# Fewer weight decodes in the retention stage, and w_in splits two chunks ahead

## The chip, the cores and the metric

The kernel runs on one core of one Trainium2 chip. The metric is device time in microseconds (us), the median of several executions. "The span" is the time from the first to the last instruction in a profiled execution.

## What is computed

Three layers, one after the other, on a batch of 4 sequences of 576 tokens (2304 tokens, 512 features):

```python
# retention: 8 heads of 64, gamma[h] = 1 - 2 ** (-5 - h)
scores = (q @ k.T) / 8                       # per batch and head
x = (scores * where(t >= s, gamma ** (t - s), 0)) @ v
x = x.transpose(0, 2, 1, 3).reshape(2304, 512)
# first feed-forward layer, w_in 512 x 2048, w_out 2048 x 512
x = relu(x @ w_in) ** 2 @ w_out
# second feed-forward layer
h = x @ w_in2
out = (h * clip(h + 3, 0, 6) / 6) @ w_out2   # output float32
```

q, k and v arrive as 32-bit floats, the four weight matrices as 64-bit floats, which the chip's engines don't compute with.

## The kernel before

**Decodes.** A weight matrix is cut into 16 chunks of 128 hidden columns. What the kernel calls a half is one chunk of one matrix, 512 KB of 64-bit words. `load_w` (L116) loads a half into a staging buffer: the first four halves have buffers of their own (t3 to t6), all later ones share three. `decode` (L132) makes 32-bit floats of it in three parts that the caller runs when it likes. The first part is two ScalarE conversions (L148, L149) and two VectorE operations (L150, L153); the second (L159) and third (L165) are VectorE's. Its two work buffers, a and r, are double. Decoded w_in chunks stay in w0 to w7, two chunks each; decoded w_out chunks go to a pool, wd.

**Splits.** Every matrix product on 32-bit floats is made of three fast ones: `split_to` (L169) writes a rounded high part (ScalarE) and the rest, the low part (VectorE or GpSimd), and TensorE runs high x high, high x low and low x high. `split_x` does that for the activations, `split_in` for a w_in chunk (into one of two buffers, q0 and q1), `split_out` for a w_out chunk.

**Retention.** 20 tiles of up to 128 tokens; the batches go in two pairs, so the tiles of index 0 to 9 are those of batches 0 and 1, and the last two of each pair have only 64 tokens. Per tile TensorE makes scores (aps, L212), an addition to the running state (sps, L233), and one tile later the values (vps, L252 and L259); VectorE masks the scores (ret, L219), adds the state (L241) and scales the result into xall (L264); GpSimd scales the tile's values (kvt, L196) and the state (L242). Five tiles' buffers are there, so the load of a tile is issued when the values of the tile five before it are done. All loads are issued by SP in the order of the program. Between the tiles, AHEAD = 8 halves of w_in are decoded: the first part in every second tile from index 2 on, the rest in the tile after it. The tile at index 11, 13, 15 and 17 also splits a quarter of the first x.

**First feed-forward layer.** 64 units: four groups of tokens (`FIRST`: 768, 512, 512, 512), 16 chunks in each. Unit i runs h = x @ w_in of its chunk (`emit_h`, 24 matmuls in the first group, 12 in the others), then g = relu(h)^2 with its split (`emit_g`), and the product with w_out of the chunk two before it (`y_steps`, LAG = 2). In the first group each unit also decodes one half of w_out and, in some units, one of w_in. The program's order on each engine is written out by hand: in a unit the decode's first part stands ahead of emit_g, the second inside it, the third behind. The loads' order is a list, `coming`; each finished decode issues the next load. In the first group h of a unit uses PSUM banks 6 and 7, which the unit before it also used, so its matmuls wait until ScalarE's ReLU (L349) has read them. Later units decode the second layer's weights (`ready_steps`) and store split weights to DRAM; the second layer (L533) follows.

## Time and profile before

| | us |
|---|---|
| median of 3 runs | 869.36 (865.73 to 869.61) |
| the profiled execution: device time | 866.37 |
| its span | 864.6 |
| TensorE busy in the span | 846.1 |
| VectorE busy | 546.3 |
| ScalarE busy | 446.8 |
| GpSimd busy | 160.2 |

The profile records one execution. PE is TensorE's matmuls, PEld its weight loads, DVE is VectorE, ACT ScalarE, POOL GpSimd, SP the queue that issues most DMAs. L12 is line 12 of the kernel. "out<-in" are the program's names of what an instruction writes and reads, "x16" the number of merged instructions. The bracket at the end of a line of the timeline is the idle time of the engine before it and what ended it. A wait for several things is put down to the one that came last. A line of the busy table has the stretch, its length, the busy time (with instructions) of PE, PEld, DVE, ACT and POOL, TensorE's granted clock as a share of full speed, the DMA engines' busy share and what they moved in GB/s. A line of the groups has busy time and mean ns of one after the first bar, idle time before them and what ended it after the second.

### The profile page before, as it was taken

How to read it: one execution, taken by the hardware profiler on the slowest of the kernel's cores; microseconds unless marked ns; L12 is line 12 of the kernel's file. 1: busy time of each engine (PE TensorE's matmuls, PEld its weight loads, DVE VectorE, ACT ScalarE, POOL GpSimd, SP SyncE). 2: the span in 40 equal slices, each digit the busy share in tenths (PEclk: the TensorE clock that was granted, in tenths of full speed). 3: DMA queues.
4: the chain of work that ended last, by engine and by line, in shares of the span. 5: the costliest groups of instructions: out<-in, count | busy, mean ns of one | idle time of the engine just before them, and what ended most of it. 6: DMA issues, size and time to landing. Idle time of an engine off the chain costs nothing.

```text
span 864.6 us, 13261 instructions
## 1 busy us (share of the span) xinstructions
PE 846.1 (98%) x4970; PEld 734.7 (85%) x4970; DVE 546.3 (63%) x888; ACT 446.8 (52%) x814; POOL 160.2 (19%) x137
## 2 busy tenths in 40 slices
PE   8987999999999999999999999999999999999998
PEld 6876788888888888888888889889989889889897
DVE  4998877765477877787675645456554455643533
ACT  1130877676576777777765533335433345433332
POOL 3444433433033313432240000000000000000000
PEclk9999999999999999999999999999999999999999
DMA  9993454545487688778768545545476453674431
GB/s 362 346 360 95 133 192 141 190 134 185 134 293 269 232 281 291 267 263 302 259 209 316 183 159 196 196 146 194 164 287 207 159 204 125 246 268 168 173 120 73
DMA packets 70576, 184.18 MB, mean 213 GB/s; under 512 B 10224, under 2 KB 26608, under 8 KB 70512
## 3 DMA queue, kind: packets, MB, share of 16 engines
q1 hardware_dynamic: 69936, 182.21, 59.9%
q10 hardware_dynamic: 576, 1.12, 0.3%
q8 instruction: 39, 0.64, 0.3%
q14 instruction: 25, 0.20, 0.1%
HBM read 147.14 MB, written 36.18 MB: 212 GB/s over the span
## 4 chain that ended last, share of the span: by engine, by line
PE 90%; DMA 4%; DVE 4%; ACT 1%; issue 1%; POOL 0%; SPq 0%; DVEq 0%; ACTq 0%; POOLq 0%
PE yps L513 23%; PE hps L329 22%; PE hps L547 20%; PE yps L372 20%; PE ytail L372 3%; DMA kvt<-in_kv_dram 2%; DVE ret L219 1%; DMA stage<-in_w_out_dram 1%; PE vps L252 1%; DVE xring L171 1%; DVE xall L264 1%; DMA cst<-in_consts_dram 1%; PE vps L259 0%; DVE a L159 0%; DVE w L165 0%
## 5 line engine op out<-in xcount | busy, mean ns | idle before, releaser
L513 PE MATMUL yps<-wo,g 128*128 128x512 f32 x864 | 226.2, 394 | 0.0
L372 PE MATMUL yps<-g,wo 128*128 128x512 f32 x768 | 194.2, 391 | 0.0
L513 PEld LDWEIGHTS yps<-wo,g 128*128 128x128 f32 x864 | 159.6, 188 | 23.6 <-DVE g L562 0.3
L372 PEld LDWEIGHTS yps<-g,wo 128*128 128x128 f32 x768 | 140.0, 188 | 24.9
L329 PE MATMUL hps<-xring,win 128*128 128x512 f32 (+1 forms) x720 | 153.7, 362 | 2.1 <-ACT r L349 2.1
L329 PEld LDWEIGHTS hps<-xring,win 128*128 128x128 f32 x720 | 123.2, 189 | 23.5 <-ACT r L349 2.3
L547 PE MATMUL hps<-xlast,win 128*128 128x384 f32 x576 | 116.1, 336 | 0.0
L547 PEld LDWEIGHTS hps<-xlast,win 128*128 128x128 f32 x576 | 103.2, 188 | 8.8
L171 DVE TENSOR_TENSOR g<-r,g 128x512 fp32r<-128x512 f32 x64 | 46.9, 733 | 82.6 <-ACT g L170 82.1
L566 DVE TENSOR_TENSOR u<-hps,u 128x384 f32<-128x384 f32 x48 | 26.8, 558 | 107.3 <-PE hps L547 107.3
L349 ACT ACTIVATE r<-hps 128x512 f32<-128x512 f32 x80 | 44.1, 552 | 95.5 <-PE hps L329 95.5
L547 PE MATMUL hps<-xop,win 128*128 128x384 f32 x432 | 87.2, 336 | 0.0
L547 PEld LDWEIGHTS hps<-xop,win 128*128 128x128 f32 x432 | 77.5, 188 | 6.6
L560 ACT ACTIVATE g<-c 128x384 fp32r<-128x384 f32 x72 | 37.8, 525 | 84.3 <-DVE c L559 84.3
L148 ACT ACTIVATE a<-stage 128x512 f32<-128x512 f32 x64 | 42.0, 656 | 45.7 <-DVE w L165 31.4
L558 ACT ACTIVATE v<-c,three 128x384 f32<-128x384 f32 x72 | 44.4, 617 | 32.6 <-DVE c L566 31.4
L329 PE MATMUL hps<-xown,win 128*128 128x512 f32 x240 | 59.8, 390 | 0.7 <-ACT xall L381 0.7
L150 DVE TENSOR_SCALAR a<-a 128x512 f32<-128x512 f32 x64 | 47.3, 739 | 10.3 <-ACT a L148 10.3
L329 PEld LDWEIGHTS hps<-xown,win 128*128 128x128 f32 x240 | 44.8, 188 | 10.1 <-ACT xall L381 0.9
L585 ACT ACTIVATE c<-hps 128x384 f32<-128x384 f32 x24 | 11.8, 492 | 76.4 <-PE hps L547 76.4
L170 ACT ACTIVATE win<-w 128x512 fp32r<-128x512 f32 x64 | 39.6, 619 | 21.4 <-PE vps L259 21.4
L559 DVE SCALAR_TENSOR_TENSOR c<-v,c 128x384 f32<-128x384 f32 x72 | 40.0, 555 | 13.7 <-ACT v L558 13.7
(75 smaller groups left out, 1042.8 us busy)
## 6 DMA issues: line engine op xcount, KB each, us to landing
wo<-kept SPq DMA_DIRECT2D x96, 512.0 KB, 5.1
win<-kept SPq DMA_DIRECT2D x72, 512.0 KB, 3.6
kept<-ready SPq DMA_DIRECT2D x40, 512.0 KB, 3.8
stage<-in_w_in_dram SPq DMA_DIRECT2D x32, 512.0 KB, 4.4
stage<-in_w_out_dram SPq DMA_DIRECT2D x32, 512.0 KB, 4.2
qkt<-in_qk_dram SPq DMA_DIRECT2D x16, 512.0 KB, 7.2
kvt<-in_kv_dram SPq DMA_DIRECT2D x16, 512.0 KB, 7.7
kept<-wo SPq DMA_DIRECT2D x16, 512.0 KB, 5.8
```

What stands on the lines that cost most here:

```text
L148: nc.scalar.activation(out=a, in_=high.bitcast(F32), func=ACTF.Abs)
L150: nc.vector.tensor_scalar(out=a, in0=a, scalar1=LEAST, scalar2=MOST, op0=ALU.max, op1=ALU.min)
L170: nc.scalar.activation(out=hi, in_=src, func=ACTF.Copy)
L171: lo_engine.tensor_tensor(out=lo, in0=src, in1=hi.bitcast(F32), op=ALU.subtract)
L329: nc.tensor.matmul(out=h, lhsT=w[:, wp, kk * 128:kk * 128 + 128], rhs=xs[pos, kk][xp][:, o:o + n], start=m == 0, stop=m == 3 * KD - 1,)
L349: nc.scalar.activation(out=r, in_=hs[k], func=ACTF.Relu)
L372: nc.tensor.matmul(out=p, lhsT=w[:, wp, m * 128:m * 128 + 128], rhs=g[pos, c][k][:, gpart, :size], start=c == 0 and e == 0 and not (k and ...
L513: nc.tensor.matmul(out=p, lhsT=gt[m // 3][:, gpart, m % 3 * 128:][:, :128], rhs=w[:, wp], start=first and e == 0, stop=last and e == 2,)
L547: nc.tensor.matmul(out=to, lhsT=wl[k][:, half, wp, o], rhs=x[:, xp, f], start=first and m == 0, stop=last and m == 5, skip_group_check=True,)
L558: nc.scalar.activation(out=v, in_=c, func=ACTF.Relu, bias=three)
L559: nc.vector.scalar_tensor_tensor(out=c, in0=v, scalar=6.0, in1=c, op0=ALU.min, op1=ALU.mult)
L560: nc.scalar.activation(out=hi, in_=c, func=ACTF.Copy)
```

## The change

- Five w_in halves are decoded in the retention tiles in place of eight: first parts at the tiles of index 4, 6, 8, 10 and 12. The other eleven follow in the units of the first group, at unit (c - 5) * 6 // 5 for chunk c.
- A decode has four parts: what was the first is now ScalarE's conversions alone, and VectorE's two operations on them are a part named clamp. In the retention tiles first and clamp run together as before. In the units, the first part is issued at the end of a unit and the rest in the next unit: w_out's at its start, that of w_in with clamp ahead of emit_g and the other two parts behind it.
- In emit_g, VectorE's low parts come after all of ScalarE's operations.
- w_in is split two units ahead in place of one: chunks 0 and 1 in the tiles of index 14 and 16, the others behind emit_g.
- Split of the second group's x comes behind emit_g in the last three units of the first group.
- The running states move from q0 to w3.
- Loads: the first five tiles are issued without halves between them, and a half follows each tile load in the tiles of index 1 to 7 (before: three halves among the first five tiles, one in each of the tiles of index 0 to 3).
- WARM, the number of matmuls on zeros at the start, goes from 26 to 18.

```diff
--- before.py
+++ after.py
@@ -33,9 +33,9 @@
 MOST = float(np.array(0x47EFFFFF, np.uint32).view(np.float32))
 LAG = 2
 
-AHEAD = 8
-
-WARM = 26
+AHEAD = 5
+
+WARM = 18
 
 READY = list(range(17, 59))
 
@@ -147,6 +147,8 @@
         def first():
             nc.scalar.activation(out=a, in_=high.bitcast(F32), func=ACTF.Abs)
             nc.scalar.activation(out=r, in_=low.bitcast(U32), func=ACTF.Copy, scale=2.0 ** -29)
+
+        def clamp():
             nc.vector.tensor_scalar(
                 out=a, in0=a, scalar1=LEAST, scalar2=MOST, op0=ALU.max, op1=ALU.min
             )
@@ -164,7 +166,7 @@
         def third():
             nc.vector.tensor_tensor(out=f.bitcast(I32), in0=a.bitcast(I32), in1=r, op=ALU.add)
 
-        return [first, second, third]
+        return [first, clamp, second, third]
 
     def split_to(hi, lo, src, lo_engine):
         nc.scalar.activation(out=hi, in_=src, func=ACTF.Copy)
@@ -173,7 +175,7 @@
 
     tiles = [(b, i, min(C, S - C * i)) for pair in range(0, B, 2) for i in range(NTB) for b in (pair, pair + 1)]
     data, rets = {}, {}
-    every = place("q0", [128, 2, 2, HP, D], F32, "state")
+    every = place("w3", [128, 2, 2, HP, D], F32, "state")
     states = [[every[:, k, j] for j in range(2)] for k in range(2)]
 
     def load_tile(ti):
@@ -336,8 +338,8 @@
 
     g, gtail = {}, []
 
-    def emit_g(pos, c, hs, between):
-        g[pos, c] = []
+    def emit_g(pos, c, hs):
+        g[pos, c], lows_g = [], []
         for k, (o, n) in enumerate(parts(pos)):
             r = cp.tile([128, 512], F32, tag="c", name="r")[:, :n]
             if k == 0:
@@ -348,11 +350,11 @@
                 gt = gtail[0][:, c % 3]
             nc.scalar.activation(out=r, in_=hs[k], func=ACTF.Relu)
             nc.scalar.activation(out=r, in_=r, func=ACTF.Square)
-            if k == 0:
-                for f in between:
-                    f()
-            split_to(gt[:, 0, :n], gt[:, 1, :n], r, nc.vector)
+            nc.scalar.activation(out=gt[:, 0, :n], in_=r, func=ACTF.Copy)
+            lows_g.append((gt[:, 1, :n], r, gt[:, 0, :n]))
             g[pos, c].append(gt)
+        for lo, src, hi in lows_g:
+            nc.vector.tensor_tensor(out=lo, in0=src, in1=hi.bitcast(F32), op=ALU.subtract)
 
     yb = {}
 
@@ -613,7 +615,7 @@
 
     halves = [(-1, 0, c, 0) for c in range(AHEAD)]
     halves += [(c, 0, c, 1) for c in range(NCH)]
-    halves += [((c - AHEAD) * 7 // 4, 0, c, 0) for c in range(AHEAD, NCH)]
+    halves += [((c - AHEAD) * 6 // 5, 0, c, 0) for c in range(AHEAD, NCH)]
     halves.sort(key=lambda x: x[0])
     coming = halves + [
         (0, 1, 2 * p + e, w) for p in range(NPAIR) for e, w in ((0, 0), (1, 0), (0, 1), (1, 1))
@@ -634,8 +636,6 @@
         load = lambda: load_w(*coming.pop(0)[1:])
         for ti in range(1, len(TOKENS)):
             load_tile(ti)
-            if ti > 1:
-                load()
 
         warm = bank(0, [128, 256], "warm")
         for _ in range(WARM):
@@ -656,10 +656,11 @@
                 scale_values(ti + 2)
             if ti:
                 values(ti - 1)
-            if ti < 4:
+            if 1 <= ti <= 7:
                 load()
-            if ti >= 2 and ti % 2 == 0 and halves[0][0] < 0:
+            if ti >= 4 and ti % 2 == 0 and halves[0][0] < 0:
                 decoding = decode(*halves.pop(0)[1:])
+                decoding.pop(0)()
                 decoding.pop(0)()
             elif decoding:
                 for f in decoding:
@@ -668,8 +669,8 @@
                 next_load()
             if ti in (11, 13, 15, 17):
                 split_x(0, (ti - 11) // 2)
-            if ti == len(tiles) - 2:
-                split_in(0, 0, nc.gpsimd)
+            if ti in (14, 16):
+                split_in(0, (ti - 14) // 2, nc.gpsimd)
         values(len(tiles) - 1)
         assert halves[0][0] >= 0 and len(xs) == KD and not decoding
         ring["from"] = 4
@@ -678,24 +679,35 @@
         ready = [f for p in range(NPAIR) for f in ready_steps(p)]
         pace, owed = sum(x[0] for x in ready) / len(READY), 0
         sums, highs, lows = operand_steps(0)
+        due = []
         for i, (pos, c) in enumerate(units):
-            dec = []
-            while halves and halves[0][0] <= i:
-                dec.append(decode(*halves.pop(0)[1:]))
             h = emit_h(pos, c)
-            if pos + 1 < len(FIRST) and c >= NCH - 3:
+            dec, due = due, []
+            for d in dec[:1]:
+                for f in d:
+                    f()
+                next_load()
+            for d in dec[1:]:
+                d.pop(0)()
+            if pos and pos + 1 < len(FIRST) and c >= NCH - 3:
                 for kk in ((0,), (1,), (2, 3))[c - NCH + 3]:
                     split_x(pos + 1, kk)
-            if i + 1 < len(units):
-                split_in(*units[i + 1], nc.gpsimd if pos == 0 else nc.vector)
+            emit_g(pos, c, h)
+            for d in dec[1:]:
+                for f in d:
+                    f()
+                next_load()
+            if pos == 0 and c >= NCH - 3:
+                for kk in ((0,), (1,), (2, 3))[c - NCH + 3]:
+                    split_x(pos + 1, kk)
+            if i + 2 < len(units):
+                split_in(*units[i + 2], nc.gpsimd if i + 2 < NCH else nc.vector)
             if 1 <= i <= NCH:
                 split_out(i - 1, nc.gpsimd)
-            for d in dec:
-                d[0]()
-            emit_g(pos, c, h, [d[1] for d in dec])
-            for d in dec:
-                d[2]()
-                next_load()
+            while halves and halves[0][0] <= i:
+                d = decode(*halves.pop(0)[1:])
+                d.pop(0)()
+                due.append(d)
             if i >= LAG:
                 for f in y_steps(*units[i - LAG]):
                     f()
```

## Rows read from the trace of the kernel before

**Rows 1.** The page, busy time and instructions of each engine, TensorE's line

```profile
PE 846.1 (98%) x4970; PEld 734.7 (85%) x4970; DVE 546.3 (63%) x888; ACT 446.8 (52%) x814; POOL 160.2 (19%) x137
```

**Rows 2.** Who waited for whom, TensorE: us in total, times, longest

```profile
PE sps L233 <- POOL kvt L196: 5.0, 6, 2.3
...
PE hps L329 <- ACT r L349: 2.1, 1, 2.1
```

**Rows 3.** Busy time by stretch, the last a chunk with two decodes

```profile
2.00:22.00 20.00, 17.14 (x219) 13.89 (x219) 8.74 (x17) 2.96 (x5) 7.34 (x9) 0.91 1.03 395
...
16.80:24.00 7.20, 6.10 (x94) 5.48 (x96) 2.61 (x6) 1.28 (x3) 3.23 (x4) 0.76 1.05 403
24.00:83.60 59.60, 51.39 (x895) 44.22 (x892) 57.64 (x92) 10.96 (x17) 28.55 (x28) 0.96 0.78 274
...
121.36:129.74 8.38, 8.38 (x51) 7.37 (x49) 6.80 (x10) 6.36 (x13) 2.87 (x3) 1.00 0.45 146
```

**Rows 4.** Timeline of TensorE: start us, us, then what

```profile
17.90 1.12 PE L233 MATMUL sps<-kvt 128*64 128x64 f32 x16 [2.30 <-POOL kvt L196]
...
62.07 1.16 PE L212 MATMUL aps<-qkt 64*128 64x128 f32 x16
63.16 0.69 PE L233 MATMUL sps<-kvt 128*64 128x64 f32 x16
63.68 1.04 PE L252 MATMUL vps<-ret,kvt 128*64 128x128 f32 x16
64.65 1.09 PE L259 MATMUL vps<-qkt,state 64*64 64x128 f32 x16
65.67 1.16 PE L212 MATMUL aps<-qkt 64*128 64x128 f32 x16
...
78.00 0.63 PE L212 MATMUL aps<-qkt 64*64 64x64 f32 x16
81.39 1.17 PE L252 MATMUL vps<-ret,kvt 64*64 64x64 f32 x15 [2.76 <-issue]
...
85.20 8.79 PE L329 MATMUL hps<-xring,win 128*128 128x512 f32 x48
```

**Rows 5.** Timeline of GpSimd, retention, fourth and eighth tile's values

```profile
16.80 1.04 POOL L196 TENSOR_TENSOR kvt<-kvt,cst 128x512 f32<-128x512 f32 x1 [3.66 <-DMA kvt<-in_kv_dram]
...
33.62 1.04 POOL L196 TENSOR_TENSOR kvt<-kvt,cst 128x512 f32<-128x512 f32 x1 [1.73 <-DMA kvt<-in_kv_dram]
```

**Rows 6.** Timeline of VectorE, retention, one decode and what follows

```profile
64.40 0.46 DVE L150 TENSOR_SCALAR a<-a 128x512 f32<-128x512 f32 x1
...
65.96 1.28 DVE L219 TENSOR_TENSOR ret<-aps,cst 128x512 f32<-128x512 f32 x2
...
68.08 0.72 DVE L159 SCALAR_TENSOR_TENSOR a<-stage,a 128x512 int32<-128x512 int32 x1
...
70.18 0.94 DVE L171 TENSOR_TENSOR xring<-xall,xring 128x768 fp32r<-128x768 f32 x1
```

**Rows 7.** Timeline of ScalarE in the first chunks, then TensorE's first y

```profile
88.42 0.60 ACT L349 ACTIVATE r<-hps 128x512 f32<-128x512 f32 x1 [0.18 <-PE hps L329]
...
91.47 0.62 ACT L170 ACTIVATE win<-w 128x512 fp32r<-128x512 f32 x1
...
93.19 0.66 ACT L148 ACTIVATE a<-stage 128x512 f32<-128x512 f32 x1
...
95.47 0.58 ACT L349 ACTIVATE r<-hps 128x512 f32<-128x512 f32 x1
...
100.40 0.86 PE L372 MATMUL yps<-g,wo 128*128 128x512 f32 x3
```

**Rows 8.** Groups by line, GpSimd, 86 to 214 us

```profile
L171 POOL TENSOR_TENSOR win<-w,win 128x512 fp32r<-128x512 f32 x16 | 26.2, 1638 | 78.6 <-ACT win L170 74.9 <-PE hps L329 3.7
```

**Rows 9.** Groups by line, VectorE, 86 to 214 us

```profile
L165 DVE CUSTOM_DVE_ANT_0 w<-a,r 128x1024 uint16<-128x1024 uint16 x8 | 13.2, 1650 | 0.0
...
L165 DVE CUSTOM_DVE_ANT_0 wd<-a,r 128x1024 uint16<-128x1024 uint16 x16 | 11.0, 685 | 0.0
```

## The prediction

> **What bounds the kernel now.** I began with the page. TensorE is busy for 846.1 of 864.6 us [rows 1], so only a stretch in which it idles, or runs at its lower clock, can give anything. The list of waits says where it idles: 5.0 us for GpSimd's scaled values (kvt) in the retention stage, and 2.1 us once at the third chunk of the first feed-forward stage [rows 2]. After that chunk the chain of waits is TensorE nearly all the way to the end, so whatever the retention stage and the first three chunks gain or lose comes out of the end one for one.
>
> The busy table by stretch then divides the retention stage in two [rows 3]. From 2 to 22 us the DMA engines are full, at 395 GB/s. Between 16.8 and 24 us VectorE works only 2.61 of 7.20 us and TensorE's granted clock is 0.76 on the mean, a mixture of its two levels, 2.4 and 1.2 GHz: both wait for tiles. From 24 to 83.6 us VectorE is busy 57.64 of 59.60 us, and is the limit; TensorE is busy 51.39 us there. The last row is a feed-forward chunk with two decodes: TensorE 8.38 of 8.38 us, VectorE 6.80, ScalarE 6.36.
>
> TensorE's order of time gives the floor [rows 4]. A full tile without delay takes 1.09 (scores) + 0.52 (state) + 0.97 + 1.02 (the two value groups) = 3.60 us, from the score start at 62.07 to the one at 65.67. But from 65.67 to the first feed-forward matmul at 85.20 it takes 19.53 us for what remains, and one of the last value groups (81.39) waited 2.76 us. At the front, the state matmuls at 17.90 waited 2.30 us for GpSimd, whose scaling of that tile began as its values landed, at 16.80 [rows 5]; those of the eighth tile landed at 33.6.
>
> VectorE's order of time prices a decode [rows 6]. Its first part pushes the next tile's masking from 64.40 to 65.96, 1.56 us; its second and third push the operand split from 68.08 to 70.18, 2.10 us: 3.66 us a decode. A tile without one takes 65.96 to 68.08, 2.12 us of VectorE, well under TensorE's 3.60.
>
> The last timeline is the change of stage [rows 7]. ScalarE's ReLU of chunk 0 starts 3.22 us after the first feed-forward matmul, its work on one chunk up to the next w_in copy takes 91.47 - 88.42 = 3.05 us, four decode conversions take 93.19 to 95.47 = 2.28 us, the ReLU of chunk 1 comes at 95.47, and the first y matmul at 100.40, 15.20 us after 85.20.
>
> **The change part by part.** The sum has three terms.
>
> *Loads (first term).* Before, w_in halves stand between the tiles in SP's order, and seven are issued before the values of the eighth tile. Afterwards the five first tiles are issued with none between, and one half follows each tile from the sixth on, so two precede the eighth tile. A half is 0.524 MB, 1.3 us at 395 GB/s [rows 3]. The fourth tile has one half less ahead of it (1.3 us earlier), the sixth and later ones four or five (5.3 to 6.6 us). TensorE can't use all of it: after the fourth tile it goes by its own 3.60 us per tile. I count 1.3 us for the earlier landing, 1.5 us because the long wait goes that pulled the clock down (7.20 us at 0.76 lose 1.7 us) [rows 3], and 0.9 us for smaller waits for GpSimd in the following tiles (5.0 us in all, 2.30 counted) [rows 2, 4]. That is -3.7 us. From there VectorE fills the time and hands the lead on unchanged, since the decodes stay at every second tile up to the thirteenth. Bounds: 0, if the first decode, which now comes at the fifth tile with a half loaded behind the sixth tile, holds VectorE until that half lands; -5.3 us, four halves. The tenth tile and on still find their loads ahead of need: their place in the queue at 395 GB/s is before VectorE's turn for them. Of the five decodes kept, each costs what it did. The decode at the third tile is dropped too, mostly inside the idle 4.59 us of the first stretch; it is counted in the 3.7.
>
> *Decodes (second term).* Those at tiles 15 and 17 go, 2 x 3.66 us of VectorE. Then VectorE needs 2.12 us per tile, about 3.1 with a split of x, so TensorE becomes the limit and the end follows its floor. From the score start at 65.67: two full tiles 7.2 us, then the two short ones and the last values. A short tile's scores take about 0.55 us (the row at 78.00, less the pipelined tail), the last full tile's values 1.99, and each of the last two value groups about 1.1 (the 1.17 of 81.39) [rows 4]: 0.55 + 1.99 + 0.55 + 1.1 + 1.1 = 5.3 us. Together 12.5 against 19.53 us: -7.0 us. It includes the 2.76 us wait, where masking stood behind a slow split. Bounds: -3.7 (one decode's worth, if the splits on VectorE and GpSimd still collide) and -8.0 (the lower clock around 81 to 85 us gone as well). The state tile moves from q0 to w3 so that the first two w_in splits can run at tiles 15 and 17 on ScalarE and GpSimd; both have room there, so nothing is charged. WARM falls by 8 matmuls, some 1.8 us of TensorE before any tile has landed: nothing either way, as tile loads set the pace; if the clock fell for it, the retention matmuls of the first three tiles would cost up to 3 us more, and this too would mostly vanish in the wait for the fourth tile.
>
> *The change of stage (third term).* In chunk 0 ScalarE now reaches its ReLU first and converts for two decodes after it. ReLU at 3.1, w_in copy at 6.2, done 6.8, four conversions 2.3: the ReLU of chunk 1 starts at 9.1 and ends at 9.7, where two chunks of matmuls end at 8.4. So TensorE waits 1.3 us in place of 2.1: -0.8. But splits two chunks ahead reuse the buffer that the running chunk reads, so in chunk 1 ScalarE copies w_in only after that chunk's ReLU work, at 9.1 + 3.05 = 12.2, done 12.8, and GpSimd's subtraction of w_in, then that of w_out(0), follow: 1.64 us for the one [rows 8] and about as much for the other, so 16.1. TensorE is at y(0) at 9.7 + 4.2 = 13.9 and runs two passes (0.5 us) before it needs the low half: it stalls 1.7 us. y(0) then stands as if begun at 15.6 against 15.2: +0.4 us. Bounds: -0.8 (no stall) and +1.5 (it waits from its first pass, or GpSimd is slowed).
>
> *Later chunks: nothing.* Chunk decodes rise from 24 to 27 and the doubles from 8 chunks to 11. A double chunk fits today [rows 3]. Splitting a decode over two chunks adds one wait: a conversion needs the buffer that the third part of the decode two earlier frees. Counting from a ReLU start: ScalarE free of g at 3.05, copies and first conversions to 5.3; VectorE's low halves, second and third part end at about 5.9, the third part held by GpSimd's subtraction of w_in; second conversions to 7.1. That is 1.3 us inside 8.38. The load of a half is issued when its buffer's reader is done and has some 6 us. The rows say how much VectorE loses when GpSimd works: the same decode's last part takes 1.65 us into w and 0.69 into wd [rows 9], and the difference goes with what GpSimd does then. Splits of x for the next stage, the copies of x, and all of the second layer keep their places behind TensorE.
>
> The Trainium skill says on its page "SBUF — State Buffer", section "SBUF: two separate sides", that VectorE and GpSimd take a shared pair of ports as an exclusive lock for a whole instruction, and that a VectorE operation with two inputs in SBUF is subject to it too. By that rule VectorE's double chunk would become its own work plus all of GpSimd's, and this speaks against moving decodes to where GpSimd is busy; read at its worst it is the second rival below, otherwise it leaves the sum as it is.
>
> **Sum.** -3.7 - 7.0 + 0.4 = -10.3 us. The profiled execution took 866.4 us (1.8 around its span), giving 856.1. The median shown, 869.4, lies 3.0 above that execution, and the three runs lie between 865.7 and 869.6; I put half of the 3.0 on top: 857.6 us.
>
> **Rivals.**
> 1. *The early lead is lost* (0.16). VectorE stands at the fifth tile until the first half lands, or DMA paces the tiles to the thirteenth as before. For it: DMA is full up to 22 us, and the half now lies behind six tiles. Against: VectorE idles 4.59 us there anyway. Time: first term 0, so -6.6, 861.3 us.
> 2. *The double chunks no longer fit* (0.10). VectorE's second and third part wait for both of GpSimd's subtractions (2 x 1.64 us, [rows 8]) in place of one, so the second conversion ends 1.6 us later, at 8.7 to 9.3, against 8.38. For it: the 1.65 us row. Against: VectorE gets in between two GpSimd operations today. Each of ten double chunks then takes 0.5 to 0.9 us more: 5 to 9 us back, 863 to 867 us: no change that counts, at its worst.
> 3. *Slower* (0.04). The same loop in ScalarE's order, with the load of a half as its last link: the load is issued only when the second part of a decode has run, and the next decode's conversion, ahead of the ReLU in ScalarE's queue, waits for it. It decides once a chunk takes over 9.4 us, 1.03 above 8.38 in ten chunks; at 10 us per chunk it costs 16 us: 874 us.
> 4. *More* (0.04): first term -5.3, second -8.0, third -0.8: 853.8 us, or less if the runs fall low.
> My forecast, -8 to -13 us, has the rest, 0.66.
>
> **Numbers.** Predicted is the likeliest, 857.6 us. Range 852.5 to 864: below by the larger bounds without the 1.5 us put on top, above by rival 1 and the milder half of rival 2. This kernel's runs tell 0.5%, about 4.3 us, from no change: faster 0.88 (forecast, rivals 1 and 4, a little of 2), same 0.08, slower 0.04.
>
> **What would show it.** Right: kvt of the eighth tile scaled near 28 us; VectorE no longer full from about 57 us; tiles 16 to 18 at 3.6 us; first feed-forward matmul near 74.5 us; a wait for ReLU of about 1.3 us at chunk 2 and one for GpSimd's w_out at y(0); after that TensorE without gaps. Wrong: a first feed-forward matmul after 80 us (first or second term), or waits of hps for ReLU in each double chunk (rivals 2 and 3).

## The result, and the profile after the change

The changed kernel takes 857.52 us, the median of four runs (856.29 to 858.22). The kernel before, on the same chip, takes 868.86 us, also over four runs (865.73 to 869.61). The ratio is 0.9875, with a 95% interval of 0.9848 to 0.9902: faster by 1.25%. The profiled execution took 857.4 us, with a span of 855.6.

The line of the page, against [rows 1]: busy time, share of the span and instructions of each engine.

```profile
PE 841.4 (98%) x4962; PEld 731.0 (85%) x4962; DVE 543.5 (64%) x889; ACT 445.4 (52%) x814; POOL 157.2 (18%) x136
```

TensorE is 4.7 us less busy than before and the span is 9.0 us shorter. The eight warm-up matmuls that were dropped are 1.7 of the 4.7 (5.73 to 4.02 us); most of the rest is time at the lower clock, and the other 4.3 us is idle time that went. Who waited for whom on TensorE, against [rows 2] (total, times, longest):

```profile
PE sps L235 <- POOL kvt L198: 3.2, 4, 1.2
...
PE aps L214 <- DMA qkt<-in_qk_dram: 1.2, 1, 1.2
```

The 5.0 us for GpSimd's values became 3.2, and the longest wait fell from 2.3 to 1.2. The wait of the third chunk for ReLU fell from 2.1 to 0.9 (the row at 85.39 below). New is 1.5 us for GpSimd's w_out (the row at 91.79), which the prediction named, and 1.2 us for the load of the eleventh tile, which it did not say; before, the only wait for a tile's load was 0.3 us, at the fourth tile.

TensorE's order of time, against [rows 4] (start, duration, and in brackets the idle time before it with its releaser):

```profile
38.19 1.16 PE L214 MATMUL aps<-qkt 64*128 64x128 f32 x16 [1.21 <-DMA qkt<-in_qk_dram]
40.56 1.06 PE L235 MATMUL sps<-kvt 128*64 128x64 f32 x16 [1.22 <-POOL kvt L198]
...
63.46 1.16 PE L214 MATMUL aps<-qkt 64*128 64x128 f32 x16
...
75.89 8.62 PE L331 MATMUL hps<-xring,win 128*128 128x512 f32 x48
85.39 4.46 PE L331 MATMUL hps<-xring,win 128*128 128x512 f32 x24 [0.88 <-ACT r L351]
...
91.79 0.50 PE L374 MATMUL yps<-g,wo 128*128 128x512 f32 x1 [1.48 <-POOL wo L173]
...
95.64 4.33 PE L331 MATMUL hps<-xring,win 128*128 128x512 f32 x24
```

The 38.19 row is the scores of the eleventh tile, 63.46 those of the seventeenth, and 75.89 the first feed-forward matmul. In what follows, h(i) and y(i) are the two products of unit i, counted from 0, so the row at 75.89 holds h(0) and h(1). From 63.46 to 75.89 are 12.43 us, against 19.53 in [rows 4]. The next three units, from 75.89 to h(3) at 95.64, take 19.75 us; before they took 19.40, from 85.20 to 104.60. After that, chunks follow each other at 8.36 to 8.39 us with no idle row.

The busy table by stretch, against [rows 3] (TensorE, weight loads, VectorE, ScalarE and GpSimd busy, then the granted clock as a share of 2.4 GHz, DMA share, GB/s):

```profile
16.80:24.00 7.20, 7.20 (x130) 6.23 (x130) 4.92 (x10) 1.26 (x2) 3.23 (x4) 1.00 1.05 404
24.00:60.00 36.00, 31.81 (x562) 27.67 (x560) 33.26 (x53) 9.09 (x14) 16.15 (x17) 0.95 1.03 370
60.00:75.90 15.90, 14.99 (x295) 13.07 (x291) 13.50 (x25) 0.00 (x0) 9.60 (x10) 1.00 0.31 83
95.60:104.00 8.40, 8.40 (x50) 7.39 (x49) 7.65 (x12) 6.06 (x13) 3.04 (x2) 1.00 0.68 216
```

The stretch from 16.8 to 24 us is at the full clock, where it was 0.76. From 24 to 60 us the DMA engines are full, and of these stretches it is the only one below the full clock, at 0.95. In the last stretch of the retention stage VectorE has time to spare, 13.50 of 15.90 us, but its first idle time comes at 67.2 us, where the prediction said about 57.

### The profile page after: what moved, and what is told of

It reads as the page before. It is cut to its first block, busy times and chain, and to the rows that moved or that the text cites. A ratio compares the mean times of both kernels' runs of the same rounds, so it can differ in the third digit from the quotient of the medians.

```text
span 855.6 us, 13276 instructions
## 1 busy us (share of the span) xinstructions
PE 841.4 (98%) x4962; PEld 731.0 (85%) x4962; DVE 543.5 (64%) x889; ACT 445.4 (52%) x814; POOL 157.2 (18%) x136
## 4 chain that ended last, share of the span: by engine, by line
PE 94%; DVE 2%; DMA 2%; ACT 1%; issue 1%; POOL 0%; SPq 0%; DVEq 0%; ACTq 0%; POOLq 0%
PE yps L515 23%; PE hps L331 22%; PE hps L549 21%; PE yps L374 20%; PE ytail L374 3%; DMA kvt<-in_kv_dram 2%; PE vps L254 1%; PE vps L261 1%; PE aps L214 1%; PE sps L235 1%; DVE ret L221 1%; DVE xring L173 0%; DVE xall L266 0%; ACT r L352 0%; POOL kvt L198 0%
## 5 line engine op out<-in xcount | busy, mean ns | idle before, releaser
L161 DVE SCALAR_TENSOR_TENSOR a<-stage,a 128x512 int32<-128x512 int32 x64 | 48.6, 759 | 1.7
L352 ACT ACTIVATE r<-r 128x512 f32<-128x512 f32 x80 | 47.2, 590 | 2.5
```

Of the source, the lines that this page charges most:

```text
L161: nc.vector.scalar_tensor_tensor(out=a.bitcast(I32), in0=high, scalar=-0x40000000, in1=a.bitcast(I32), op0=ALU.bitwise_and, op1=ALU.bitwis ...
L352: nc.scalar.activation(out=r, in_=r, func=ACTF.Square)
```

## The experiments

Edits are to the changed kernel unless another base is named. Each ratio is to the kernel before in the same batch. That kernel's own median moved between batches (870.5 for the first four experiments, 866.5 for the next four, then 868.7, and 867.9 for the last), so ratios of different batches can differ by up to 0.5% for no reason in the kernel. Places in the profile (the first feed-forward matmul) were compared first, but each is from a single execution, which need not be a typical one; executions of one and the same retention code put it up to 1.7 us apart (see the part on the prediction).

### What the order of the loads is worth

**e2_old_loads** puts the loads back into the old order.

```diff
             load_tile(ti)
+            if ti > 1:
+                load()
...
-            if 1 <= ti <= 7:
+            if ti < 4:
                 load()
```

> The changed kernel with the load order of before (three halves among the first five tiles, one behind each of the tiles of index 0 to 3). Theory (the first term is real): the fourth tile waits for its values again, the lead of 2.2 us at the thirteenth tile goes, first feed-forward matmul near 78.1 us, span near 857.8. Rival (the lead is lost by the thirteenth tile whatever the loads do, and the gain comes from the dropped decodes alone): 75.9 and 855.6.

Ratio 0.9879 (0.9863 to 0.9896), 859.77 us. TensorE's order of time, the seventeenth tile's scores and the first feed-forward matmul:

```profile
66.80 1.16 PE L214 MATMUL aps<-qkt 64*128 64x128 f32 x16
...
79.23 8.67 PE L331 MATMUL hps<-xring,win 128*128 128x512 f32 x48
```

The end of the stage is unchanged, 12.43 us. All of the loss up to here, 3.34 us against the profiled execution of the changed kernel, lies ahead of the seventeenth tile. (The profiled execution took 861.1 us, 1.3 above the median.) The new order is worth something there. The size is looked at again below.

**e6_start2** keeps the old loads and lets the five decodes begin two tiles earlier (`if ti >= 2` in place of `ti >= 4`, on top of e2_old_loads).

> The load order of before and the five decodes from the tile of index 2 on (2 to 10), all else as in the changed kernel. With the old loads and decodes at 4 to 12 the first feed-forward matmul came at 79.2 us, with the changed loads at 75.9, and in the kernel before with five decodes at 2 to 10 at 76.1. Theory (the load order only pays back the later start of the decodes): 75.5 to 76.7, span 855 to 856.5, as the changed kernel. Rival (the load order is a gain of its own): 78 or later, span over 857.5.

Ratio 0.9905 (0.9889 to 0.9922), 858.46 us; the first feed-forward matmul is at 77.17, between the two expectations. By these profiles two tiles earlier are worth 2.1 us (79.23 to 77.17), so part of what the new loads give would only pay back the later start of the decodes. It isn't shown beyond this pair: e2's profiled execution lies 1.3 us above its median and e6's 0.5 above, and the ratios (0.9879 and 0.9905) go the other way.

**e1_spread_loads** spreads the halves out (`if ti <= 13 and ti % 2: load()`), because the lead got in the front was not kept. VectorE's masking of the fifth tile starts 4.9 us ahead of before (18.92 against 23.84), that of the ninth 5.1, that of the eleventh 4.2, the twelfth 3.0, the thirteenth 2.2, and from there on it stays. VectorE's order of time, the masking of the ninth and thirteenth tile, before and then in the changed kernel with its one idle time between them:

```profile
40.05 0.87 DVE L219 TENSOR_TENSOR ret<-aps,cst 64x256 f32<-64x256 f32 x2
...
53.50 1.28 DVE L219 TENSOR_TENSOR ret<-aps,cst 128x512 f32<-128x512 f32 x2
```

```profile
34.92 0.86 DVE L221 TENSOR_TENSOR ret<-aps,cst 64x256 f32<-64x256 f32 x2
...
43.58 0.42 DVE L266 TENSOR_TENSOR xall<-vps,cst 128x256 f32<-128x256 f32 x1 [0.99 <-PE vps L261]
...
51.32 1.27 DVE L221 TENSOR_TENSOR ret<-aps,cst 128x512 f32<-128x512 f32 x2
```

GpSimd's order of time, the eleventh and thirteenth tile's values before, then the eighth, eleventh and thirteenth in the changed kernel:

```profile
42.87 1.04 POOL L196 TENSOR_TENSOR kvt<-kvt,cst 128x512 f32<-128x512 f32 x1 [1.85 <-DMA kvt<-in_kv_dram]
...
47.89 1.27 POOL L196 TENSOR_TENSOR kvt<-kvt,cst 128x512 f32<-128x512 f32 x1 [0.38 <-DMA kvt<-in_kv_dram]
```

```profile
28.13 1.04 POOL L198 TENSOR_TENSOR kvt<-kvt,cst 128x512 f32<-128x512 f32 x1 [2.12 <-DMA kvt<-in_kv_dram]
...
39.47 1.04 POOL L198 TENSOR_TENSOR kvt<-kvt,cst 128x512 f32<-128x512 f32 x1 [2.57 <-DMA kvt<-in_kv_dram]
...
47.07 1.04 POOL L198 TENSOR_TENSOR kvt<-kvt,cst 128x512 f32<-128x512 f32 x1 [2.11 <-DMA kvt<-in_kv_dram]
```

The eighth tile's values are scaled at 28.13, 5.5 us earlier than in [rows 5]. But from there up to 47 us each scaling starts as the values land, 3.5 to 4.3 us apart, and the lead of the landing shrinks: 5.5 us at the eighth tile, 3.4 at the eleventh, 0.8 at the thirteenth. The scores at 38.19 and the state matmuls at 40.56 (shown above) waited 1.21 and 1.22 us. With the halves moved ahead of them, the tiles from the eleventh on are late.

> The changed kernel with its seven halves loaded behind the tiles of index 1, 3, 5 ... 13 in place of 1 to 7. In the changed kernel VectorE's masking leads that of before by 5.1 us at the ninth tile but only by 2.2 at the thirteenth. Theory (loads): the halves that stand between the tiles in the full DMA queues hold the tenth to thirteenth tile back. With fewer of them there about 2.5 us of the lead stays: first feed-forward matmul near 73.5 us (changed kernel 75.9), span near 853.2 (855.6). Rival (GpSimd): the lead is lost because VectorE's decode parts and split wait behind GpSimd's scaling; then nothing moves: 75.5 to 76.2 and 855.2 to 856.

Ratio 0.9831 (0.9813 to 0.9850), 855.5 us. The result is mixed. The profiled execution (857.0 us, 1.5 above the median) has its first feed-forward matmul at 75.32, just ahead of the rival's range; the median is nearer to the theory. VectorE is without idle time from 29.4 to 61 us, and the stretch from the ninth tile's masking to the thirteenth's took 13.89 us in place of 16.40, so the loads did hold these tiles back. But the ninth tile's masking came 1.9 us later (36.80). At the start the scores of the second tile took 2.08 us at a granted clock of 0.50, and the fifth tile's masking was 0.9 us late; then decode parts took longer beside GpSimd, as the last part at 48.58 with 1.32 us. The changed kernel has such parts too (1.45 us at 39.61): GpSimd is a second limit.

### Whether the spread over two chunks is needed

**e3_five_only** is the kernel before with nothing but the five decodes and their due times.

```diff
-AHEAD = 8
+AHEAD = 5
...
-    halves += [((c - AHEAD) * 7 // 4, 0, c, 0) for c in range(AHEAD, NCH)]
+    halves += [((c - AHEAD) * 6 // 5, 0, c, 0) for c in range(AHEAD, NCH)]
```

> The kernel before with only the number of decodes in the retention stage changed, five in place of eight (at the tiles of index 2 to 10), the other eleven w_in decodes at the same units as in the changed kernel, but whole within one unit; splits one unit ahead, loads, warm-up and state buffer as before. Theory (the second term is the dropped decodes alone): VectorE is no longer the limit from the tile of index 12 on, first feed-forward matmul at 74 to 76 us, and the chunks hold TensorE's pace, span 854 to 856. Rival (the spread over two chunks is needed): the first five chunks, double and whole, make the h matmuls wait for ReLU by 0.5 us or more each beside the 2.1 us of before, span 857 to 860.

Ratio 0.9873 (0.9856 to 0.9889), 859.21 us. TensorE's order of time:

```profile
63.62 1.16 PE L212 MATMUL aps<-qkt 64*128 64x128 f32 x16
...
76.05 8.62 PE L329 MATMUL hps<-xring,win 128*128 128x512 f32 x48
86.81 6.03 PE L329 MATMUL hps<-xring,win 128*128 128x512 f32 x24 [2.14 <-ACT r L349]
...
96.88 4.34 PE L329 MATMUL hps<-xring,win 128*128 128x512 f32 x24
...
105.26 4.34 PE L329 MATMUL hps<-xring,win 128*128 128x512 f32 x24
```

and, for comparison, h(2) in the kernel before:

```profile
96.11 4.45 PE L329 MATMUL hps<-xring,win 128*128 128x512 f32 x24 [2.12 <-ACT r L349]
```

The end of the stage again takes 12.43 us, and the first feed-forward matmul comes at 76.05, as early as in the changed kernel. The chunks from h(3) hold 8.38 us with eleven doubles, unspread. Only the first three are worse, 20.83 us: the wait for ReLU is 2.14, and the matmuls that follow it took 6.03 us where they take 4.46 in the changed kernel. The busy table says why:

```profile
87.00:90.00 3.00, 3.00 (x8) 2.32 (x9) 2.97 (x7) 2.68 (x6) 0.15 (x1) 0.50 0.13 25
```

TensorE worked 0.86 of the 3.00 us up to 87, and in the 3.00 after that its granted clock was 0.50, the lower of its two levels. In the kernel before, the same wait of 2.12 us was followed by 4.45 us at the full clock. So taking three decodes out of the retention tiles brings most of the gain: 11.3 us of some 13.8 in this batch (870.5 to 859.21, and an estimate of 856.7 for the changed kernel from e4, below). The spread over two chunks isn't needed to make the double chunks fit. At the change of stage e3 is 1.1 us behind (20.83 against 19.75), but the fall of the clock, 1.6 us, is more than that, so what the spread and the earlier splits bring there isn't shown.

### The change of stage and the room in the chunks

**e4_wout_first** puts the split of w_out ahead of that of w_in in each unit.

```diff
-            if i + 2 < len(units):
-                split_in(*units[i + 2], nc.gpsimd if i + 2 < NCH else nc.vector)
             if 1 <= i <= NCH:
                 split_out(i - 1, nc.gpsimd)
+            if i + 2 < len(units):
+                split_in(*units[i + 2], nc.gpsimd if i + 2 < NCH else nc.vector)
```

> The changed kernel with the split of w_out placed ahead of the split of w_in in every unit. Theory: the 1.5 us that the first y waits for GpSimd is GpSimd's order alone, since the w_in split in front of it waits for the running chunk's matmuls and ReLU; it goes, span near 854.1 (855.6), first feed-forward matmul unchanged at 75.9. Rival: the wait only moves to the h of a later chunk, which waits for w_in's low part or for ReLU: span 855.3 to 856.

Ratio 0.9828 (0.9812 to 0.9844), 855.05 us. TensorE's order of time:

```profile
74.48 8.65 PE L331 MATMUL hps<-xring,win 128*128 128x512 f32 x48
84.01 4.45 PE L331 MATMUL hps<-xring,win 128*128 128x512 f32 x24 [0.88 <-ACT r L351]
...
92.56 4.34 PE L331 MATMUL hps<-xring,win 128*128 128x512 f32 x24
```

From the first feed-forward matmul to h(3) are 18.08 us in place of 19.75. The wait at y(0) is gone, that for ReLU is the same 0.88, and nothing is late in its place. The third term's mechanism, w_out behind w_in on GpSimd, is shown. It is also the cheapest improvement found.

**e7_one_more** and **e8_two_more** ask how much room ScalarE has in a chunk. They run the conversions of one more decode in each unit (e7), or of every decode twice (e8); the repeated ones write the same values again.

```diff
             while halves and halves[0][0] <= i:
                 d = decode(*halves.pop(0)[1:])
+                if not due:
+                    d[0]()
                 d.pop(0)()
```

> The changed kernel with ScalarE's two conversions of the w_out half run twice in every unit of the first group (1.1 us more of ScalarE per chunk, the same values written again). Theory (a double chunk has 1.3 us to spare in ScalarE's order): nothing, span 855 to 856.5. Rival (the double chunks have nothing to spare, as the waits for VectorE of 2.2 and 2.5 us in that order suggest): h waits for ReLU in most double chunks, 0.5 us or more each, span over 860.

> The same with every decode's conversions run twice in the first group's units (2.3 us more of ScalarE in a double chunk). Theory (1.3 us to spare): 1.0 us too much in each of ten double chunks, less what single chunks give back: span 860 to 866. Rival (the extra conversions fall into the waits for VectorE and cost less): span 855.5 to 859.

e7: ratio 0.9896 (0.9880 to 0.9912), 857.73 us. The wait at h(2) is 1.98 in place of 0.88, h(3) comes 20.86 us after the first feed-forward matmul, and then chunks take 8.38 us without a wait. The 1.1 us of two conversions cost 1.1 once and nothing later. That it would cost nothing at all was wrong.

e8: ratio 0.9923 (0.9904 to 0.9942), 860.13 us. The span, 856.9, is in the rival's range: the extra conversions cost much less than 1.0 us in each double chunk. One such chunk by the busy table:

```profile
104.75:113.26 8.51, 8.51 (x50) 7.29 (x49) 7.39 (x11) 8.38 (x17) 3.33 (x2) 1.00 0.63 186
```

ScalarE is now busy 8.38 us, and this chunk and the next take 8.51 and 8.54 in place of 8.38: this is the point at which ScalarE's own work decides. Four more conversions start about 0.57 us apart, 2.27 us, so that work takes 8.53 - 2.27 = 6.26 us in the changed kernel, which leaves 2.1 us. With its waits for VectorE ScalarE has less to spare. Its order of time in the changed kernel:

```profile
91.76 0.58 ACT L351 ACTIVATE r<-hps 128x512 f32<-128x512 f32 x1
...
99.21 0.68 ACT L148 ACTIVATE a<-stage 128x512 f32<-128x512 f32 x1 [2.21 <-DVE w L167]
...
100.36 0.58 ACT L351 ACTIVATE r<-hps 128x512 f32<-128x512 f32 x1
...
107.38 0.58 ACT L351 ACTIVATE r<-hps 128x512 f32<-128x512 f32 x1
```

and VectorE's second and third part just before the conversion at 99.21:

```profile
95.69 1.79 DVE L161 SCALAR_TENSOR_TENSOR a<-stage,a 128x512 int32<-128x512 int32 x1
97.52 1.66 DVE L167 CUSTOM_DVE_ANT_0 w<-a,r 128x1024 uint16<-128x1024 uint16 x1
```

The conversion at 99.21 waited 2.21 us for VectorE's third part, the wait that the prediction added. The two parts, 0.69 us each where GpSimd is idle, stood beside GpSimd's two subtractions (95.44 to 96.94 and 96.89 to 98.63). So this ReLU comes 8.60 us after the one before it, longer than the 8.38 of a chunk, and the next 7.02 us later; the one after that (116.26) takes 8.88. On the mean of four chunks, from 84.76 to 116.26, it is 7.88 us, with no wait for TensorE. ScalarE stays ahead, and TensorE isn't held. With e7's extra conversions these waits for VectorE are gone for three chunks, and the ReLUs follow at 7.4 us (85.69 to 107.88).

### Which limit comes next in the retention tiles

**e5_four** decodes four halves in the tiles, on top of e4_wout_first.

```diff
-AHEAD = 5
+AHEAD = 4
...
-    halves += [((c - AHEAD) * 6 // 5, 0, c, 0) for c in range(AHEAD, NCH)]
+    halves += [((c - AHEAD) * 11 // 10, 0, c, 0) for c in range(AHEAD, NCH)]
```

> Four w_in halves in the retention stage in place of five (the tiles of index 4 to 10; chunk c from 4 on at unit (c - 4) * 11 // 10), and w_out split ahead of w_in as in the run before. Theory (VectorE with its decodes sets the pace up to the last one, TensorE's 3.60 us per tile after it): 3.7 us of VectorE go from the thirteenth and fourteenth tile, first feed-forward matmul at 71.5 to 73 us (74.5 in the run with w_out first), span 850 to 851.5. Rival (the loads or TensorE already set the pace there, or the extra decode makes a chunk too long): no gain, span 852.5 to 855.

Ratio 0.9855 (0.9835 to 0.9876), 854.85 us: no gain over e4_wout_first. TensorE's order of time at the eleventh and twelfth tile, and the busy table there:

```profile
38.86 1.16 PE L214 MATMUL aps<-qkt 64*128 64x128 f32 x16 [1.95 <-DMA qkt<-in_qk_dram]
41.45 1.12 PE L235 MATMUL sps<-kvt 128*64 128x64 f32 x16 [1.43 <-POOL kvt L198]
...
44.40 2.08 PE L214 MATMUL aps<-qkt 64*128 64x128 f32 x16
```

```profile
42.00:44.00 2.00, 2.00 (x40) 1.88 (x38) 0.42 (x1) 1.19 (x2) 0.15 (x1) 0.50 1.03 420
```

With less for VectorE the tiles reach their loads sooner, and wait longer: 1.95 and 1.43 us. Then the twelfth tile's scores take 2.08 us, since the granted clock is 0.50 from 42 to 46 us. The rival, the loads, is right: with the halves in this order, the saved decode is lost to them and to the clock.

**e9_four_spread** adds e1's spread loads to e5_four. **e10_five_spread** is the same with five decodes.

> Both at once: four halves in the retention stage, their loads behind the tiles of index 1, 3, 5 ... 13, w_out split first. With four halves alone the eleventh tile waited 2.0 us for its load and TensorE's clock fell; with spread loads alone VectorE had no idle time and stayed the limit. Theory (two limits stand side by side from the tenth to the fourteenth tile, loads and VectorE, and one alone gives nothing): together first feed-forward matmul at 71.5 to 73 us (75.3 and 75.3 alone), span 850 to 851.5. Rival (TensorE or GpSimd is a third limit there): 74 to 75.5, span 852.5 to 854.

> Five halves, loads spread, w_out split first: the run above with one decode more. Theory (two limits): VectorE stays the limit, first feed-forward matmul 74 to 75.5 us, span 852.5 to 854; it lies 1.5 us or more above the run with four. Rival (the loads were the only limit, and the first look at spread loads was an unlucky execution): 72 to 73.5 us, span 850.5 to 852.

e9: ratio 0.9820 (0.9799 to 0.9841), 853.46 us, first feed-forward matmul at 73.49, between theory and rival. e10: 0.9837 (0.9815 to 0.9859), 854.67 us, at 73.11, in the rival's range. So the spread helps with four decodes (73.49 against 75.27, and 71.82 in e11 below). With five it isn't told: e10's profile is 1.4 us ahead of e4's (74.48), its ratio no better (0.9828). Whether the fifth decode still costs anything can't be told either: the profiles and the medians of e9 and e10 differ by 0.4 and 1.2 us in opposite directions.

**e11_warm26** is e9 with WARM back at 26.

> The run with four halves and spread loads with the 26 warm-up matmuls of before in place of 18. In the executions of the changed kernel some of the first two tiles' scores took 1.8 to 2.1 us in place of 1.16, as they do at the lower clock. Theory (warm-up is hidden by the loads up to the fourth tile): within 0.5 us of the run with 18. Rival (the lower clock there costs what it shows): the third tile's scores up to 0.9 us earlier and the span as much shorter.

Ratio 0.9823 (0.9800 to 0.9846), 853.02 us; the scores of the third tile start at 11.82 against 11.90. The warm-up matmuls aren't seen, as the prediction said. The first feed-forward matmul comes at 71.82, 1.67 us ahead of e9's, though the two run the same from the third tile on and still lie 0.08 us apart at the ninth tile's scores (32.32 and 32.40); e9's profiled execution lies 0.5 us above its median, e11's 1.1 below.

**e12_no_scaling** is e9 without GpSimd's scaling of the values; the output is then not the reference's.

```diff
     def scale_values(ti):
-        n = tiles[ti][2]
-        kvt = data[ti][1]
-        nc.gpsimd.tensor_tensor(
-            out=kvt[:, 1], in0=kvt[:, 1],
-            in1=(gv if n == C else gw).unsqueeze(2).to_broadcast([128, H, D]), op=ALU.mult,
-        )
+        pass
```

> The kernel with four halves and spread loads, without GpSimd's scaling of each tile's values (the values are left unscaled, so the output is not the reference's). VectorE was busy 39.8 of 42 us from 22 to 58 us there, less idle only behind waits for GpSimd's instructions. Theory (GpSimd is the limit that is left from the seventh to the thirteenth tile, by holding VectorE's decode parts): decode parts fall from 1.2 and 1.3 to 0.5 to 0.7 us, the masking of the thirteenth tile comes at 47.5 us or before (50.5), first feed-forward matmul at 70 to 72 us (73.5), span 848.5 to 850.5. Rival (loads or TensorE): the masking stays after 49 us, first feed-forward matmul at 72.5 us or later.

Ratio 0.9811 (0.9782 to 0.9840), 851.68 us, first feed-forward matmul at 69.75: just beyond the theory's range. Against e9's 73.49 that is 3.7 us, against e11's 71.82, which has the scaling too, 2.1. The span gains less, 849.6 against 852.2 and 850.2, since one load in the second layer came 1.3 us late; and the ratios of the three don't tell them apart. The masking of the thirteenth tile comes at 46.73, as the theory said (50.48 in e9, 48.82 in e11). VectorE's groups from 22 to 58 us (busy, mean ns of one, then the idle time before), e9_four_spread:

```profile
L221 DVE TENSOR_TENSOR ret<-aps,cst 128x512 f32<-128x512 f32 x16 | 10.2, 678 | 0.0
...
L167 DVE CUSTOM_DVE_ANT_0 w<-a,r 128x1024 uint16<-128x1024 uint16 x4 | 4.7, 1171 | 0.6
L161 DVE SCALAR_TENSOR_TENSOR a<-stage,a 128x512 int32<-128x512 int32 x4 | 3.5, 869 | 0.0
L155 DVE TENSOR_SCALAR a<-a 128x512 int32<-128x512 int32 x4 | 3.2, 797 | 0.1
```

e11_warm26, the same code but for the warm-up:

```profile
L161 DVE SCALAR_TENSOR_TENSOR a<-stage,a 128x512 int32<-128x512 int32 x4 | 3.8, 942 | 0.0
...
L167 DVE CUSTOM_DVE_ANT_0 w<-a,r 128x1024 uint16<-128x1024 uint16 x4 | 2.8, 692 | 0.5
...
L155 DVE TENSOR_SCALAR a<-a 128x512 int32<-128x512 int32 x4 | 1.7, 427 | 0.1
```

and e12_no_scaling (where the masking has line 216):

```profile
L216 DVE TENSOR_TENSOR ret<-aps,cst 128x512 f32<-128x512 f32 x18 | 11.5, 682 | 0.4 <-PE aps L209 0.4
...
L161 DVE SCALAR_TENSOR_TENSOR a<-stage,a 128x512 int32<-128x512 int32 x4 | 2.8, 692 | 0.0
L167 DVE CUSTOM_DVE_ANT_0 w<-a,r 128x1024 uint16<-128x1024 uint16 x4 | 2.8, 692 | 0.5
...
L155 DVE TENSOR_SCALAR a<-a 128x512 int32<-128x512 int32 x4 | 1.7, 428 | 0.1
```

With the same operands, these three decode operations take 2.84 us per decode in e9 and 1.81 without the scaling. But in e11, with the scaling, they take 2.06: two of the three are as short as in e12, and only the second part (L161) is long. So what GpSimd's scaling costs VectorE depends on which instruction it meets, and that differs between executions of the same code. The masking (ret), with one operand in PSUM, does not change: 678 and 682 ns, and e9's at 52.61 took 1.28 us for its two instructions with GpSimd at work in 1.21 of them. The state matmuls' wait for scaled values is gone in e12 too, so not all of the 2.1 to 3.7 us is proven to be VectorE's.

## Why the prediction was right, and where it was off

**The sum.** By the 17th tile's scores, the first feed-forward matmul and h(3), the terms in the profiled execution are:

| term | predicted, us | measured, us | from |
|---|---|---|---|
| loads | -3.7 | -2.2 | 65.67 [rows 4] to 63.46 |
| decodes | -7.0 | -7.1 | 19.53 to 12.43 |
| change of stage | +0.4 | +0.35 | 19.40 to 19.75 |
| later chunks | 0 | 0 | 8.38 each |
| sum | -10.3 | -9.0 | span 864.6 to 855.6 |

**Loads: the term that was mis-sized.** The mechanism was there: the fourth and fifth tile come early, the 2.30 us wait is gone, the clock from 16.8 to 24 us is 1.00, the eighth tile's values come at 28.13 (near 28 was said). At the ninth tile the lead is 5.1 us, close to the bound of 5.3. What failed is the step by which VectorE "hands the lead on unchanged": from the ninth tile's masking to the thirteenth's it took 16.40 us in place of 13.45 (the rows under e1_spread_loads).

First, "The tenth tile and on still find their loads ahead of need": the eleventh waited 1.21 and 1.22 us, and e5_four shows 1.95 and 1.43 when VectorE asks sooner. The halves are only put off. In the order of the program four fewer stand ahead of the sixth to ninth tile (not "four or five"; ahead of the eighth tile's loads there were six before, not seven), but three, two, one and none ahead of the tenth, eleventh, twelfth and thirteenth. At 1.3 us each that would be leads of 5.3 us down to none, and the values landed 5.5, 3.4 and 0.8 us earlier at the eighth, eleventh and thirteenth tile. Meanwhile VectorE's need had moved forward by 5 us. TensorE's late tile then left VectorE idle for 0.99 us.

Second, "Of the five decodes kept, each costs what it did": all five together do (15.84 us of VectorE against 15.83, each part at its own length), but not each. Those at the fifth and seventh tile fell from 4.00 and 3.21 to 2.40 and 2.97, and those at the ninth and eleventh, where the lead was lost, rose from 2.42 and 2.57 to 3.31 and 3.53, with GpSimd beside them. The idle time and these two rises are 2.8 of the 2.95 us.

The term isn't one number either: the retention stage with the same code took the seventeenth tile's scores to 63.46, 62.05, 63.26 and 61.78 in four executions (the changed kernel, e4, e7, e8), so -2.2 to -3.9, -3.0 on the mean. They part at the eleventh tile. The busy table, the changed kernel and then e8_two_more:

```profile
42.00:44.00 2.00, 2.00 (x34) 1.88 (x32) 1.00 (x4) 2.00 (x4) 0.83 (x1) 0.50 1.07 411
```

```profile
42.00:44.00 2.00, 1.28 (x24) 1.02 (x18) 1.73 (x3) 1.98 (x3) 1.07 (x2) 1.00 1.06 417
```

The granted clock was 0.50 in the changed kernel and in e7, and 1.00 in e8 and e4; the state matmuls began at 40.41 to 40.56 in all four, the twelfth tile's scores at 43.46 and 43.12 against 42.12 and 42.10. Where the clock held, the term is -3.6 and -3.9, the predicted size; where it fell, -2.2 and -2.4. The prediction counted 1.5 us for a fall of the clock that goes, and none for a new one.

**Decodes.** As predicted, in every kernel with five: TensorE's floor of 12.43 us from the seventeenth tile's scores, also with the old loads and the unspread decodes. The state tile and the two early splits cost nothing there.

**Change of stage.** Right with both of its parts: the wait for ReLU was 0.88 (1.3 predicted, 2.1 before), the one for w_out's low half 1.48 (1.7 predicted), and e4_wout_first removed the second alone, for -1.67. The two effects nearly cancel, so the net is small for a change of that much order.

**Later chunks.** No cost, as predicted, though the chain was closer to its limit than was said. The added wait for the third part exists (2.21 us at 99.21) and was hidden. From ReLU to ReLU the chain took 7.02 us in one chunk, near the 7.1 of the prediction, and 8.60 and 8.88 in those beside it, where VectorE's second and third part stood beside both of GpSimd's subtractions. That is the mechanism of rival 2, in every other chunk; on the mean it took 7.88 us, under the 8.38, so its price did not come. Rival 3 did not show. The Trainium skill, on its page "SBUF — State Buffer", section "SBUF: two separate sides", says that a GpSimd operation and a VectorE operation that needs the shared ports exclude each other for a whole instruction. The trace agrees where VectorE's operation reads SBUF alone (1171 against 692 ns for the third part in e9 and e12, 1.79 and 1.66 us in the rows above), and the operation that reads PSUM and one tile of SBUF kept its 678 to 682 ns. It was felt in the tiles and, without a cost to TensorE, in the chunks.

**The total.** 857.52 against 857.6 is closer than the steps deserve, and in part luck. The sum was 1.3 us too good (856.1 against 857.4 for a profiled execution), and the 1.5 us put on top was not there, since the changed kernel's median lies on its profiled execution (857.52 and 857.4) while that of before lies 2.5 above its own. The two errors cancel, and a profile in which the clock held at the eleventh tile would have come out 1.4 to 1.7 us lower.

**What stays open.** Why the clock fell at the eleventh tile in two of four executions: the two waits ahead of it were 1.21 and 1.22 us where it fell in the changed kernel, and 1.50 and 1.29 where it held in e8. How much of the loads' term belongs to the order and how much to the spread between executions: e2_old_loads is 3.3 us behind one profile and 5.0 behind another. With e4_wout_first's 1.67 us taken back, e4 gives an estimate of 856.7 us for the changed kernel in e2's own batch, and e2 took 859.77: about 3 us. Whether four or five decodes are best with spread loads isn't settled. The best version that computes the reference is e9_four_spread or, not to be told from it, e11_warm26, at a ratio of 0.982.

## What to carry to other kernels

When an engine that fills a stage is relieved, price the relieved stretch by the floor of the next engine, read from tiles where that engine already runs without waits: this gave -7.0 for -7.1. When loads are reordered so that work starts earlier, count for every later tile what now stands ahead of its load, and move its need by the same lead, before saying that the load is in time. When the same code scatters between executions, find the row at which two of them part before giving a term one number. Changes of stage are worth an order of their own: there, exchanging two splits on GpSimd gave 1.67 us for two lines moved.

## What the runs showed of the hardware

- One and the same retention code differed by 1.7 us between executions (seventeenth tile's scores at 61.78 to 63.46), on a stage of 75 us; most of it, 1.0 to 1.4 us, came with a granted clock of 0.50 in place of 1.00 from 42 to 44 us.
- After waits of 1.8 to 3.4 us in all, TensorE ran at a granted clock of 0.50 for some us (e3 from 87 to 90, e5 from 42 to 46, e1 from 8 to 11), and matmul groups of 1.16 us took 2.08. A wait can cost more than its length, but need not: 2.14 us ahead of h(2) in e3 were followed by 6.03 us of matmuls, 2.12 us at the same place in the kernel before by 4.45.
- VectorE's operations on SBUF alone took up to 1.9 times as long when GpSimd worked beside them (797 against 428 ns on the mean for one of them), and those with an operand in PSUM took the same (678 and 682). The same operations took 427 ns in e11, with the same work on GpSimd: it depends on what meets what.
